# A scan followed by two gated layers: GpSimd adds the last three bits of all seventeen weight groups, and the order of work is drawn up anew

## The chip, the cores and the metric

The kernel runs on one core of one Trainium2 chip. The metric is the device time of one execution in microseconds (us): the median of three timed runs. One further execution was recorded by the hardware profiler, and all rows come from that one. In what follows PE is TensorE (PEld its weight loads), DVE is VectorE, ACT is ScalarE, POOL is GpSimd and SP is SyncE, which issues the transfers.

## The reference

A chunked linear recurrence over 768 steps for 4 batches of 8 heads makes `x`, 3072 tokens of 256 features. Two layers follow:

```python
h = x @ w_in                                   # 256 -> 2048
g = np.where(h > 0, h, np.exp(np.minimum(h, 0)) - 1)
x = g @ w_out                                  # 2048 -> 256
out = ((x @ w_a) * (x @ w_b)) @ w_out2         # 256 -> 1536 -> 256
```

[...]

## The kernel before

**The work.** Tokens are cut into 6 tiles of 512, and the recurrence into 24 units of 128 steps, 4 units to a tile. Stage A computes the first layer tile by tile: for each tile 8 pairs (`pair`), each with two blocks of 128 of the 2048 hidden features. A pair multiplies by `w_in` into PSUM (`up_a`, or `up_q` in the first two pairs, which take half a tile at a time), goes through ACT and DVE (`ex`, `em`, `gg`), and multiplies by `w_out` (`down`). Tile 0 multiplies by the whole 32-bit weights; from tile 1 on, weights and activations are split into a high and a low part of the faster type `fp32r` (`split`, `hi`, `lo`), and three products stand for one. Stage B computes the second layer for two tiles at a time in 18 groups (`group`).

**The units.** Each unit (`unit`) loads its data, scans on DVE (L678), multiplies on PE (`cbm2` L719, `ym` L766 to L774), masks on DVE (L735) and copies its result to `x0` on ACT (L806). For units 0 to 3 the scan reads a row that PE has spread over the partitions (`spread`, L654). GpSimd makes `xe` (L698), `sbd` (L750) and `cd` (L756) for them. Units 0 to 3 must be complete before tile 0 is.

**The weights.** There are 17 groups of 1024 columns: `w_in` and `w_out` have four each (numbers 0 to 7, in the order `w_in` 0, `w_out` 0, `w_in` 1, `w_out` 1, and so on), and `w_a`, `w_b` and `w_out2` three each (8 to 16). `weight` takes the two 32-bit words of each number through these steps: `load` (SP); `scale` (L523) on the upper word and `last3` (L536), which brings the top three bits of the lower word down to the end, both on ACT as the order stands; `shift` (L528) and `sign` (L531) on DVE; and `put` (L541), an integer addition that adds those last three bits. `PUT_DVE[n]` names the engine of the `put` of group n: 0 is GpSimd, 1 is VectorE, 2 either. VectorE has it for n = 2, 4 and 6, which are `w_in` 1, 2 and 3. Tile 0 multiplies by the result `m` directly: `w_in` 1 from pair 2 on (blocks 4 to 7), `w_in` 2 from pair 4, `w_in` 3 from pair 6.

**The order.** Each engine works through a queue in the order in which instructions were issued to it. `Plan` draws the order up when the kernel is built. Each step has its engines with an estimated cost, the steps it depends on, a due time, and for some a time before which it may not start. The planner repeatedly takes the step that could start first, in slots of 0.25 us, and among these the one with the lowest due time. It treats the port that DVE and POOL share as held by one of them at a time, for steps with `port=True`, of which `put` is one. `MOVE` adds an amount to due times, under "" for a whole part and by a step's name for one step. Where PE would wait early in the plan, `plan.fill` issues small multiplications of zeros (`warm`, L417) to fill the wait.

Of the kernel before, what the change touches and what calls it, by code (L numbers as in the profile page):

```python
# [35 lines left out]

LO_DVE = [[0, 1, 0, 1, 0, 1, 0, 1]] * NTILE

PUT_DVE = [0, 0, 1, 0, 1, 0, 1, 0, 0, 0, 0, 0, 0, 0, 0, 0, 0]
REST_DVE = [1, 1, 1, 1, 0, 1, 0, 1, 1, 0, 1, 0, 1, 0, 1, 0, 1]  # L40

T1, PAIR1, PAIR, GROUP = 25.0, 8.0, 6.2, 14.96
# [4 lines left out]


MOVE = {
    ("bc", (0, 1, 1)): {"": 7.7, "cast": 5.0},  # L50
    ("bc", (0, 2, 0)): {"": -5.4, "load": 2.3, "rest": -6.3},
# [4 lines left out]
    ("group", 1): {"dn_h": -2.5, "dn_l": -2.0, "lo": 6.2, "mm3": -0.9},  # L56
    ("group", 10): {"": 4.8, "hi": -4.1, "lo": -1.1},
    ("group", 11): {"ad": -4.1},
    ("group", 14): {"dn_l": -0.8, "lo": -5.3, "mm3": 1.4},
    ("group", 16): {"": 0.6},  # L60
    ("group", 17): {"dn_l": 1.7, "mm3": -2.1},
    ("group", 2): {"gg": -0.9, "mm3": 1.1},
    ("group", 3): {"dn_h": -1.4, "dn_l": 2.8, "lo": 2.7, "mm3": 1.7},
    ("group", 4): {"": 0.8, "hi": -2.2, "lo": 1.7, "mm3": 2.5},
    ("group", 5): {"": -8.2, "cp": 0.2, "dn_h": 0.5},
    ("late", 0): {"comb": 2.6},
    ("late", 1): {"": 0.1},
    ("late", 3): {"": -10.3},
    ("late", 4): {"high": 3.0},
    ("late", 5): {"": 3.5, "high": 9.5},  # L70
    ("late", 6): {"": 8.5, "high": -13.9},
    ("late", 7): {"": -14.4, "comb": 10.6},
    ("late", 8): {"": 0.3, "high": -6.8},
    ("pair", (0, 0)): {"": -7.7},
    ("pair", (0, 5)): {"": -2.6},
    ("pair", (0, 7)): {"": 2.8},
    ("pair", (1, 0)): {"": 4.8},
    ("pair", (1, 2)): {"up_a": 1.7},
    ("pair", (1, 7)): {"up_a": -1.9},
    ("pair", (2, 0)): {"": -10.6, "gg": 1.7},  # L80
    ("pair", (2, 1)): {"": 3.4, "up_a": -1.2},
    ("pair", (2, 2)): {"": 6.9},
    ("pair", (2, 3)): {"": -2.2, "dn_l": -1.2},
    ("pair", (2, 4)): {"": 1.7, "hi": -4.5, "lo": 3.7},
    ("pair", (2, 5)): {"": -3.8, "dn_l": -5.9, "lo": -0.2, "up_a": -2.2},
    ("pair", (2, 6)): {"": -4.1},
    ("pair", (2, 7)): {"up_a": -5.2},
    ("pair", (3, 2)): {"": 6.7, "dn_h": -3.4},
    ("pair", (3, 3)): {"": 4.4, "dn_h": -2.6},
    ("pair", (3, 4)): {"": 5.2, "up_a": -1.9},  # L90
    ("pair", (3, 5)): {"": -15.0, "dn_h": 2.3, "up_a": 1.0},
    ("pair", (3, 6)): {"": 6.9, "dn_h": -4.6, "up_a": -1.4},
    ("pair", (3, 7)): {"": 6.8, "dn_h": 13.1},
    ("pair", (4, 0)): {"": 9.0},
    ("pair", (4, 1)): {"": -11.8},
    ("pair", (4, 3)): {"": -11.1, "dn_h": -2.5, "dn_l": 3.6},
    ("pair", (4, 4)): {"": -0.6, "up_a": 5.5},
    ("pair", (4, 6)): {"dn_l": -5.5, "hi": 3.0},
    ("pair", (4, 7)): {"": -5.4, "em": 2.7, "up_a": -1.2},
    ("pair", (5, 0)): {"": 5.7},  # L100
    ("pair", (5, 1)): {"up_a": -3.1},
    ("pair", (5, 3)): {"up_a": -7.0},
    ("pair", (5, 4)): {"up_a": 0.1},
    ("pair", (5, 5)): {"": 5.8},
    ("pair", (5, 6)): {"": 4.7, "up_a": -6.5},
    ("pair", (5, 7)): {"": -0.7, "dn_h": 3.4},
    ("split", ("w_in", 0)): {"high": -20, "rest": -2.9},
    ("split", ("w_in", 1)): {"": -1.8, "high": -2.8},
    ("split", ("w_in", 3)): {"": 6.1, "high": 3.2},
    ("split", ("w_out", 0)): {"": 1.5},  # L110
    ("split", ("w_out", 1)): {"": -8.2},
    ("unit", 0): {"": 8.5, "ld0": -15.4, "ld_x": -9.9, "mask": -5.0},
    ("unit", 1): {"ld0": 7.0, "ld_x": 13.0},
    ("unit", 10): {"ld_a": -20, "st_bd": -5.0},
    ("unit", 11): {"scan": 6.0, "st_up": 8.5},
    ("unit", 12): {"": -12.6, "ld_a": 5.9},
    ("unit", 13): {"": -7.7, "<lambda>": 3.6, "scan": -4.3},
    ("unit", 14): {"": -0.6, "ld_sm": 4.0, "scan": -2.6, "st_bd": -4.2},
    ("unit", 15): {"": -3.8, "<lambda>": 11.8, "cbm": 6.9, "ld_a": 18.7, "scan": 5.9},
    ("unit", 16): {"": -8.1, "st_bd": -7.0},  # L120
    ("unit", 17): {"": -9.6, "last_col": 17.8},
    ("unit", 18): {"scan": 6.9, "st_bd": 10.0},
    ("unit", 19): {"": 6.4, "cbm": 8.3, "st_bd": -16.1},
    ("unit", 2): {"ld0": 12.2},
    ("unit", 20): {"": -4.8, "<lambda>": -18.3, "ld_db": -6.6, "ld_x": -2.5, "scan": 9.0},
    ("unit", 21): {"": 5.1, "ld_x": -4.6, "mask": 8.5, "scan": -4.0},
    ("unit", 22): {"<lambda>": 14.0, "cbm": -2.1, "ld_a": -9.9, "scan": 1.5, "x_lo": 15.3},
    ("unit", 23): {"mask": 7.9, "scan": 4.2, "st_bd": -12.9},
    ("unit", 3): {"ld_x": 12.1},
    ("unit", 5): {"last_col": 16.9, "x_hi": 20},  # L130
    ("unit", 6): {"": 2.8, "<lambda>": 6.4, "ld_a": -5.0, "ld_x": 2.7},
    ("unit", 7): {"": 3.0, "<lambda>": -1.2, "ld_a": -1.9, "ld_x": -3.6, "st_bd": -0.4},
    ("unit", 8): {"": 10.9, "ld_a": -7.3, "scan": -4.6, "st_up": 6.9, "x_lo": 3.9, "xend": -3.1},
    ("unit", 9): {"": 2.0, "ld_a": -3.0, "ld_sm": 2.5},
    ("w", ("w_in", 1)): {"shift": -19.7},
    ("w", ("w_in", 2)): {"put": 8.6},
    ("w", ("w_in", 3)): {"": 4.1, "scale": 7.8},
    ("w", ("w_out", 1)): {"put": -20, "sign": -11.6},
    ("w", ("w_out", 2)): {"sign": -6.5},
    ("w", ("w_out", 3)): {"load": -16.2, "sign": 4.2},  # L140
    ("wb", ("w_a", 0)): {"": -0.2, "last3": 7.5, "load": 0.2},
    ("wb", ("w_a", 1)): {"": -11.5},
    ("wb", ("w_a", 2)): {"": 12.0, "shift": -2.6, "sign": -2.6},
    ("wb", ("w_b", 0)): {"": -8.4, "scale": -20, "sign": -6.0},
    ("wb", ("w_b", 1)): {"": -8.8, "last3": 18.2, "shift": 18.2},
    ("wb", ("w_b", 2)): {"": 10.0, "last3": -3.0, "load": 7.0, "sign": 15.3},
    ("wb", ("w_out2", 0)): {"": 4.1, "sign": -9.5},
    ("wb", ("w_out2", 1)): {"sign": 6.5},
    ("wb", ("w_out2", 2)): {"last3": 13.0, "load": 16.4, "put": 10.3, "scale": 12.6, "shift": -0.1, "sign": -3.4},
    ("xset", 1): {"": -11.8, "x_h": -13.3, "x_l": 0.9},  # L150
}


# [13 lines left out]
class Plan:  # L167
# [12 lines left out]
    def add(self, engines, fn, *after, due, port=False, pad=0.0, weight=1.0, nb=0.7):  # L180
        flat = []
        name = fn.__name__
        move = MOVE.get(self.part, {})
        move = move.get("", 0.0) + move.get(name, 0.0)
        due, nb = due + move, nb + move if nb != 0.7 else nb
        self.parts.append((self.part, name))
        for a in after:
            flat += a if isinstance(a, list) else [a]
        self.steps.append((engines, fn, [a for a in flat if a is not None], due, port, pad, weight, nb))
        return len(self.steps) - 1  # L190
# [96 lines left out]
def kernel(  # L287
# [205 lines left out]
    def weight(name, g, due, now=True):  # L493
# [54 lines left out]
        wm[key] = m  # L548
        i_m[key] = add(({"POOL": 2.5}, {"DVE": 1.32}, {"DVE": 1.32, "POOL": 2.5})[PUT_DVE[n]], put, i4, i5, due=due, port=True)
        rb.users += [i1, i4, i_m[key]]  # L550
# [949 lines left out]
```

## Time and profile before

| quantity | value |
| --- | --- |
| timed runs, median (lowest to highest) | 619.58 us (619.28 to 619.68) |
| the profiled execution: its time, its span | 619.26 us, 617.2 us |
| busy: PE, DVE, ACT, POOL | 610.4, 393.8, 372.5, 332.4 us |
| mean granted clock of TensorE | 0.999 |

The span runs from the first instruction to the last, and 2.06 us of the execution's time lie outside it. PE's multiplications overlap and their ends are modelled, so that a busy PE may still be one that does less than it could. The chain of waits tells better when PE was held up by another engine.

### The profile page before, as it was taken

How to read it: one execution, taken by the hardware profiler on the slowest of the kernel's cores; microseconds unless marked ns; L12 is line 12 of the kernel's file. 1: busy time of each engine (PE TensorE's matmuls, PEld its weight loads, DVE VectorE, ACT ScalarE, POOL GpSimd, SP SyncE). 2: the span in 40 equal slices, each digit the busy share in tenths (PEclk: the TensorE clock that was granted, in tenths of full speed). 3: DMA queues.
4: the chain of work that ended last, by engine and by line, in shares of the span. 5: the costliest groups of instructions: out<-in, count | busy, mean ns of one | idle time of the engine just before them, and what ended most of it. 6: DMA issues, size and time to landing. Idle time of an engine off the chain costs nothing.

```text
span 617.2 us, 9444 instructions
## 1 busy us (share of the span) xinstructions
PE 610.4 (99%) x3627; PEld 482.3 (78%) x3627; DVE 393.8 (64%) x534; ACT 372.5 (60%) x529; POOL 332.4 (54%) x250
## 2 busy tenths in 40 slices
PE   9999999999999999999999999999999999999997
PEld 8875457778787877877888888888888888888885
DVE  7878768788778878878545647656533446433334
ACT  3555767766776766657777555556555556545453
POOL 2423367565555564356354576666655666555542
PEclk9999999999999999999999999999999999999999
DMA  7949633676677836410000000000100000100001
GB/s 230 308 171 306 204 95 125 229 251 234 206 256 249 293 107 214 135 52 0 2 1 1 1 0 1 0 1 1 69 0 2 0 1 0 70 0 1 1 0 68
DMA packets 33404, 59.94 MB, mean 97 GB/s; under 512 B 2736, under 2 KB 13904, under 8 KB 33360
## 3 DMA queue, kind: packets, MB, share of 16 engines
q1 hardware_dynamic: 33360, 59.35, 29.4%
q8 instruction: 28, 0.46, 0.3%
q14 instruction: 16, 0.13, 0.1%
HBM read 47.61 MB, written 11.73 MB: 96 GB/s over the span
## 4 chain that ended last, share of the span: by engine, by line
PE 98%; DVE 0%; ACT 0%; issue 0%; POOL 0%; POOLq 0%
PE acc L857 6%; PE acc L853 6%; PE up L841 6%; PE up L842 6%; PE acc L854 6%; PE up L844 6%; PE up L1183 5%; PE up L1182 5%; PE up L1186 5%; PE up L832 5%; PE acc L832 5%; PE acc L1243 4%; PE acc L1242 4%; PE acc L1244 4%; PE ybank L1243 3%; PE cbank L1243 3%
## 5 line engine op out<-in xcount | busy, mean ns | idle before, releaser
L1271 DVE TENSOR_TENSOR x<-x 128x512 f32<-128x512 f32 x36 | 30.3, 847 | 68.0 <-POOL x L1315 67.6
L940 ACT ACTIVATE e<-up 128x1024 f32<-128x1024 f32 x44 | 45.1, 1026 | 40.6 <-PE up L844 27.8
L1277 POOL TENSOR_TENSOR gl<-x,gh 128x512 fp32r<-128x512 f32 x35 | 48.4, 1385 | 37.7 <-ACT gh L1274 34.4
L961 POOL TENSOR_TENSOR gl<-e,gh 128x1024 fp32r<-128x1024 f32 x20 | 50.9, 2547 | 27.9 <-ACT gh L954 21.9
L1315 POOL TENSOR_TENSOR x<-e,x 128x512 f32<-128x512 f32 x36 | 46.8, 1316 | 34.1 <-ACT e L1254 33.3
L853 PE MATMUL acc<-gh,hi_w_out 128*128 128x512 f32 x160 | 63.5, 397 | 0.0
L854 PE MATMUL acc<-gh,lo_w_out 128*128 128x512 f32 x160 | 62.4, 390 | 0.0
L944 ACT ACTIVATE e<-e,bias 128x1024 f32<-128x1024 f32 x44 | 50.8, 1153 | 0.9
L857 PE MATMUL acc<-gl,hi_w_out 128*128 128x512 f32 x160 | 51.1, 396 | 0.0
L678 DVE TENSOR_TENSOR_SCAN ab<-ab,delta 128x512 f32<-128x512 f32 x36 | 50.1, 1410 | 1.2 <-DMA ab<-a_seg 1.2
L541 POOL TENSOR_TENSOR m<-m,raw 128x1024 int32<-128x1024 int32 x11 | 26.8, 2433 | 25.7 <-DVE m L531 11.4
L841 PE MATMUL up<-xh,hi_w_in 128*128 128x512 f32 x96 | 39.3, 409 | 0.0
L950 DVE SCALAR_TENSOR_TENSOR up<-e,up 128x512 f32<-128x512 f32 x40 | 27.7, 694 | 17.7 <-ACT e L944 17.0
L1262 DVE TENSOR_TENSOR p<-acc,p 128x512 f32<-128x512 f32 x36 | 24.3, 688 | 21.7 <-PE acc L1244 19.3
L1183 PE MATMUL up<-gh,lo_w_out 128*128 128x512 f32 x96 | 37.5, 391 | 0.0
L1182 PE MATMUL up<-gh,hi_w_out 128*128 128x512 f32 x96 | 37.5, 391 | 0.0
L950 DVE SCALAR_TENSOR_TENSOR e<-e,up 128x512 f32<-128x512 f32 x48 | 30.6, 678 | 10.8 <-ACT e L944 10.8
L1262 DVE TENSOR_TENSOR x<-acc,x 128x512 f32<-128x512 f32 x36 | 23.9, 685 | 21.3 <-PE acc L1244 21.2
L842 PE MATMUL up<-xh,lo_w_in 128*128 128x512 f32 x96 | 37.4, 390 | 0.0
L1274 ACT CAST gh<-x 128x512 fp32r<-128x512 f32 x36 | 22.4, 622 | 24.4 <-DVE x L1271 24.4
L1277 POOL TENSOR_TENSOR gl<-p,gh 128x512 fp32r<-128x512 f32 x18 | 23.9, 1331 | 21.8 <-issue 21.8
L853 PEld LDWEIGHTS acc<-gh,hi_w_out 128*128 128x128 f32 x160 | 30.1, 188 | 6.0
(306 smaller groups left out, 1733.7 us busy)
## 6 DMA issues: line engine op xcount, KB each, us to landing
ab<-a_seg SPq DMA_DIRECT2D x18, 512.0 KB
parts<-raw SPq DMA_DIRECT2D x64, 128.0 KB
sm<-parts SPq DMA_DIRECT2D x16, 512.0 KB
p<-in_xb SPq DMA_DIRECT2D x20, 256.0 KB
raw<-in_w_out SPq DMA_DIRECT2D x4, 1024.0 KB
fx<-in_w_out SPq DMA_DIRECT2D x3, 1024.0 KB
out_t<-m SPq DMA_DIRECT2D x12, 256.0 KB
raw<-in_w_in SPq DMA_DIRECT2D x2, 1024.0 KB
```

The lines of the kernel that those rows point to most:

```text
L832: nc.tensor.matmul(ps, w_mm(name, wm, f, c), src, start=start, stop=stop)
L841: nc.tensor.matmul(ps, w_mm(name, whi, f, c), xh[:, c, :], start=(c == 0), stop=False)
L842: nc.tensor.matmul(ps, w_mm(name, wlo, f, c), xh[:, c, :], start=False, stop=False)
L853: nc.tensor.matmul(accs[m], w_mm(name, whi, f, m), gh, start=(f == 0), stop=False)
L854: nc.tensor.matmul(accs[m], w_mm(name, wlo, f, m), gh, start=False, stop=False)
L857: nc.tensor.matmul(accs[m], w_mm(name, whi, f, m), gl, start=False, stop=(f == last))
L950: nc.vector.scalar_tensor_tensor(u[:, k, :] if on_dve else gf[:, k, :], gf[:, k, :], 0.0, u[:, k, :], op0=ALU.min, op1=ALU.max)
L961: nc.gpsimd.tensor_sub(gl.ap, gf, gh.ap.bitcast(F32))
L1182: nc.tensor.matmul(a4[m].ap, w_mm("w_out2", whi, f, m), gh, start=first, stop=False)
L1183: nc.tensor.matmul(a4[m].ap, w_mm("w_out2", wlo, f, m), gh, start=False, stop=False)
L1243: nc.tensor.matmul(bk.ap, lo_, x[:, 0], start=False, stop=False, **on)
L1277: eng[e].tensor_sub(tap("l" + w), tap(wa), tap("h" + w).bitcast(F32))
```

## The change

`PUT_DVE` is now zero for all groups: GpSimd does every `put`, among them the three that VectorE did. `MOVE` is replaced as a whole by another table, so that due times all over the kernel differ. No function, cost estimate or dependence changes. The core of the diff, with the lines that the prediction speaks of:

```diff
-PUT_DVE = [0, 0, 1, 0, 1, 0, 1, 0, 0, 0, 0, 0, 0, 0, 0, 0, 0]
+PUT_DVE = [0] * 17
...
-    ("pair", (0, 0)): {"": -7.7},
+    ("pair", (0, 0)): {"": -9.3},
...
-    ("unit", 0): {"": 8.5, "ld0": -15.4, "ld_x": -9.9, "mask": -5.0},
-    ("unit", 1): {"ld0": 7.0, "ld_x": 13.0},
-    ("unit", 2): {"ld0": 12.2},
-    ("unit", 3): {"ld_x": 12.1},
+    ("unit", 0): {"ld0": -8.0},
+    ("unit", 1): {"": 1.9, "scan": -1.2},
+    ("unit", 2): {"": 16.2},
+    ("unit", 3): {"": -5.0, "ld_x": 10.5},
...
-    ("w", ("w_in", 1)): {"shift": -19.7},
-    ("w", ("w_in", 2)): {"put": 8.6},
-    ("w", ("w_in", 3)): {"": 4.1, "scale": 7.8},
+    ("w", ("w_in", 0)): {"last3": -2.0},
+    ("w", ("w_in", 1)): {"": -14.5, "load": 3.3, "scale": 18.2, "sign": 7.3},
+    ("w", ("w_in", 2)): {"shift": 5.3, "sign": 5.5},
+    ("w", ("w_in", 3)): {"": 8.4, "load": -1.6, "shift": 1.6},
+    ("w", ("w_out", 0)): {"": -13.7, "shift": -7.1},
...
```

The rest of the table has some 120 lines before and after, for the units of later tiles, the pairs, the splits, the weights of the second layer and the groups of stage B, with amounts of up to 20 on either side.

## Rows read from the trace of the kernel before

**Rows 1.** The page: busy time by engine; the chain that ended last, by engine.

```profile
PE 610.4 (99%) x3627; PEld 482.3 (78%) x3627; DVE 393.8 (64%) x534; ACT 372.5 (60%) x529; POOL 332.4 (54%) x250
...
PE 98%; DVE 0%; ACT 0%; issue 0%; POOL 0%; POOLq 0%
```

**Rows 2.** The chain in order of time: start us, length us, what.

```profile
24.95 1.94 PE up L832 x8
...
27.97 0.86 ACT e L944
...
29.22 0.28 ACT x L806
...
29.54 1.50 PE ybank L417 x24
31.04 1.78 PE up L832 x8
...
612.83 0.59 ACT m L1211
```

**Rows 3.** Groups by line, PE: busy us, mean ns, idle before with its releasers.

```profile
L417 PE MATMUL ybank<-zt 128*128 128x128 bf16 x135 | 10.1, 241 | 1.9 <-POOL zt L413 1.1 <-ACT x L806 0.8
```

**Rows 4.** Line 541, the put: lowest, median and highest ns, first and last start.

```profile
L541 POOL TENSOR_TENSOR m<-m,fx x3: 2398/2398/2400, 26.2 to 83.4; 128x1024 int32<-128x1024 int32 x3
L541 DVE CUSTOM_DVE_ANT_0 m<-fx,m x2: 1216/1220/1225, 31.6 to 56.1; 128x2048 uint16<-128x2048 uint16 x2
L541 DVE CUSTOM_DVE_ANT_0 m<-raw,m x1: 1192/1192/1192, 73.2 to 73.2; 128x2048 uint16<-128x2048 uint16 x1
```

**Rows 5.** Timeline of POOL: start us, length us, what, idle before with its releaser.

```profile
26.18 2.40 POOL L541 TENSOR_TENSOR m<-m,fx 128x1024 int32<-128x1024 int32 x1 [1.21 <-issue]
...
37.88 0.62 POOL L698 TENSOR_TENSOR xe<-p,le 128x256 f32<-128x256 f32 x1 [8.43 <-ACT le L693]
...
53.19 0.62 POOL L750 TENSOR_TENSOR sbd<-state,hmask 128x256 f32<-128x256 f32 x1 [3.74 <-PE ybank L766]
...
58.80 0.74 POOL L698 TENSOR_TENSOR xe<-f_lo_w_out,le 128x256 f32<-128x256 f32 x1 [4.58 <-ACT le L693]
...
74.22 0.68 POOL L698 TENSOR_TENSOR xe<-f_lo_w_out,le 128x256 f32<-128x256 f32 x1 [5.44 <-ACT le L693]
```

**Rows 6.** Timeline of DVE.

```profile
24.53 1.52 DVE L531 SCALAR_TENSOR_TENSOR m<-fx,m 128x1024 int32<-128x1024 int32 x1
25.97 0.68 DVE L735 TENSOR_TENSOR f_lo_w_out<-cbank,f_lo_w_out 128x512 f32<-128x512 f32 x1
...
27.17 1.97 DVE L528 TENSOR_SCALAR m<-m 128x1024 int32<-128x1024 int32 x1
...
30.36 1.22 DVE L531 SCALAR_TENSOR_TENSOR m<-fx,m 128x1024 int32<-128x1024 int32 x1
...
51.59 1.20 DVE L531 SCALAR_TENSOR_TENSOR m<-fx,m 128x1024 int32<-128x1024 int32 x1
...
56.13 1.22 DVE L541 CUSTOM_DVE_ANT_0 m<-fx,m 128x2048 uint16<-128x2048 uint16 x1
...
58.40 0.67 DVE L528 TENSOR_SCALAR m<-m 128x1024 int32<-128x1024 int32 x1
...
70.96 1.21 DVE L531 SCALAR_TENSOR_TENSOR m<-raw,m 128x1024 int32<-128x1024 int32 x1
```

**Rows 7.** Timeline of PE: where tile 0 comes to its later blocks.

```profile
39.03 1.98 PE L832 MATMUL up<-x,m 128*128 128x512 f32 x4
...
58.96 5.31 PE L832 MATMUL up<-x,m 128*128 128x512 f32 x12
...
64.20 0.43 PE L766 MATMUL ybank<-f_lo_w_out,sbd 128*32 128x128 f32 x8
...
77.01 1.88 PE L832 MATMUL up<-x,m 128*128 128x512 f32 x4
```

**Rows 8.** Timeline of ACT: the first step of `w_out` 0.

```profile
17.44 1.14 ACT L523 ACTIVATE m<-fx 128x1024 f32<-128x1024 f32 x1 [2.09 <-DMA fx<-in_w_out]
```

More of the change, by code (lines that the diff above doesn't have):

```diff
@@ L49 @@
 MOVE = {
-    ("bc", (0, 1, 1)): {"": 7.7, "cast": 5.0},
-    ("bc", (0, 2, 0)): {"": -5.4, "load": 2.3, "rest": -6.3},
[4 rows of a table removed]
[L56 to L73, printed above, removed]
-    ("pair", (0, 0)): {"": -7.7},
-    ("pair", (0, 5)): {"": -2.6},
-    ("pair", (0, 7)): {"": 2.8},
@@ L77 @@
[L77 to L111, printed above, removed]
@@ L112 @@
-    ("unit", 0): {"": 8.5, "ld0": -15.4, "ld_x": -9.9, "mask": -5.0},
-    ("unit", 1): {"ld0": 7.0, "ld_x": 13.0},
[L114 to L120, printed above, removed]
@@ L121 @@
-    ("unit", 17): {"": -9.6, "last_col": 17.8},
-    ("unit", 18): {"scan": 6.9, "st_bd": 10.0},
-    ("unit", 19): {"": 6.4, "cbm": 8.3, "st_bd": -16.1},
-    ("unit", 2): {"ld0": 12.2},
[L125 to L128, printed above, removed]
@@ L129 @@
-    ("unit", 3): {"ld_x": 12.1},
[L130 to L134, printed above, removed]
-    ("w", ("w_in", 1)): {"shift": -19.7},
-    ("w", ("w_in", 2)): {"put": 8.6},
-    ("w", ("w_in", 3)): {"": 4.1, "scale": 7.8},
@@ L138 @@
[L138 to L150, printed above, removed]
+    ("bc", (0, 1, 0)): {"": -5.4},
+    ("bc", (0, 2, 0)): {"": -9.9, "rest": -7.9},
+    ("bc", (0, 2, 1)): {"rest": -9.9},
+    ("bc", (1, 2, 0)): {"": -6.8, "cast": 16.2},
+    ("bc", (1, 2, 1)): {"": 3.0, "cast": 3.2, "rest": 5.8},
@@ new lines @@
+    ("group", 0): {"": -2.1, "cp": 1.5, "dn_1": 0.9, "dn_h": 2.3, "dn_l": 2.2, "mm3": -2.4},
+    ("group", 1): {"": -9.0, "gg": 3.0, "lo": 11.1, "mm3": -1.0},
+    ("group", 10): {"mm3": -0.8},
+    ("group", 11): {"lo": 1.9},
+    ("group", 17): {"dn_h": 4.2},
+    ("group", 2): {"dn_h": -2.3, "dn_l": -4.2},
+    ("group", 4): {"": 2.7, "gg": 1.4},
+    ("group", 5): {"dn_l": -1.5},
+    ("group", 6): {"": -6.8},
+    ("late", 0): {"": -6.2, "high": 3.2},
+    ("late", 1): {"": 16.7, "comb": -5.2, "high": 3.2},
@@ new lines @@
+    ("late", 3): {"": 2.7, "comb": -6.0, "high": 3.2, "high_s": 7.0, "rest_s": 5.0},
+    ("late", 5): {"": -3.1, "high": -7.9},
+    ("late", 6): {"": 6.0, "rest": 0.6},
+    ("late", 7): {"": -17.6, "high": 8.0},
+    ("late", 8): {"": 0.4, "high": -2.9},
+    ("pair", (0, 0)): {"": -9.3},
+    ("pair", (0, 3)): {"": 6.9},
+    ("pair", (0, 4)): {"": -3.9, "dn_w": 5.2},
+    ("pair", (1, 2)): {"up_a": 2.8},
+    ("pair", (1, 4)): {"": -2.8},
+    ("pair", (1, 5)): {"": -6.3, "dn_h": 1.7},
+    ("pair", (1, 6)): {"": -6.0},
@@ new lines @@
+    ("pair", (2, 0)): {"": -11.5},
+    ("pair", (2, 1)): {"dn_h": -0.2, "dn_l": -1.6},
+    ("pair", (2, 2)): {"lo": 4.1},
+    ("pair", (2, 3)): {"": 2.5, "dn_l": -0.9},
+    ("pair", (2, 4)): {"": 6.5, "dn_l": -3.2, "lo": 3.7},
+    ("pair", (2, 5)): {"": -10.0, "em": 4.9},
+    ("pair", (2, 6)): {"": -4.3},
+    ("pair", (3, 1)): {"": 2.1},
+    ("pair", (3, 3)): {"dn_h": -1.1},
+    ("pair", (3, 4)): {"": 5.2},
+    ("pair", (3, 5)): {"": -18.0},
+    ("pair", (3, 6)): {"dn_h": -3.1, "up_a": -1.1},
@@ new lines @@
+    ("pair", (3, 7)): {"dn_h": 14.4},
+    ("pair", (4, 0)): {"": 3.6},
+    ("pair", (4, 1)): {"": -18.1},
+    ("pair", (4, 3)): {"": -3.8},
+    ("pair", (4, 4)): {"": -5.2, "dn_h": -1.2},
+    ("pair", (4, 5)): {"": 4.8, "dn_h": 1.7},
+    ("pair", (4, 6)): {"": 2.8, "up_a": -2.4},
+    ("pair", (4, 7)): {"up_a": -1.8},
+    ("pair", (5, 1)): {"": -3.7},
+    ("pair", (5, 2)): {"": 13.2},
+    ("pair", (5, 6)): {"": 5.0},
+    ("split", ("w_in", 0)): {"": -4.8, "high": -15.7, "rest": 3.1},
@@ new lines @@
+    ("split", ("w_in", 3)): {"": 5.8, "high": 5.5},
+    ("split", ("w_out", 0)): {"": 9.6, "high": -11.1},
+    ("split", ("w_out", 2)): {"": -5.5},
+    ("unit", 0): {"ld0": -8.0},
+    ("unit", 1): {"": 1.9, "scan": -1.2},
+    ("unit", 11): {"": 1.9, "scan": 5.5, "ym": -7.9},
+    ("unit", 12): {"": -19.8, "ld_a": 20},
+    ("unit", 13): {"": -12.1, "mask": -5.6},
+    ("unit", 14): {"st_bd": -4.0},
+    ("unit", 15): {"cbm": -3.7, "ld_x": -1.8, "mask": -10.3},
+    ("unit", 16): {"": -2.5, "last_col": 16.5, "mask": 4.1, "st_bd": -18.9},
@@ new lines @@
+    ("unit", 17): {"": -6.5, "ym": 3.2},
+    ("unit", 18): {"": -16.0, "st_bd": 18.9},
+    ("unit", 19): {"": 3.3, "ld_a": -7.5, "x_lo": -10.5},
+    ("unit", 2): {"": 16.2},
+    ("unit", 20): {"": -4.9, "mask": 10.7},
+    ("unit", 21): {"cbm": -4.8, "st_bd": -3.0, "x_lo": 6.2, "ym": -10.4},
+    ("unit", 22): {"": -17.0, "mask": -11.1, "scan": -4.5},
+    ("unit", 23): {"cbm": -5.8, "ld_a": 4.2, "mask": 16.6, "scan": 2.1},
+    ("unit", 3): {"": -5.0, "ld_x": 10.5},
+    ("unit", 4): {"": -6.5},
@@ new lines @@
+    ("unit", 5): {"": -1.0, "ld_db": 6.8, "ld_x": 13.1, "scan": 2.8},
+    ("unit", 6): {"": 5.2, "<lambda>": 10.3, "ld_a": -7.9, "scan": 5.0},
+    ("unit", 7): {"": 3.8, "ld0": -3.1, "ld_a": -3.5, "ld_db": -7.0, "ld_x": -2.6, "scan": 1.1},
+    ("unit", 8): {"": 11.2, "ld_a": -9.6, "ld_db": 1.8, "st_bd": 4.2},
+    ("unit", 9): {"": 2.0, "ld_a": -8.3, "ld_x": -0.6, "mask": -11.4},
+    ("w", ("w_in", 0)): {"last3": -2.0},
+    ("w", ("w_in", 1)): {"": -14.5, "load": 3.3, "scale": 18.2, "sign": 7.3},
@@ new lines @@
+    ("w", ("w_in", 2)): {"shift": 5.3, "sign": 5.5},
+    ("w", ("w_in", 3)): {"": 8.4, "load": -1.6, "shift": 1.6},
+    ("w", ("w_out", 0)): {"": -13.7, "shift": -7.1},
+    ("w", ("w_out", 1)): {"": -16.7, "put": -1.0, "sign": -20},
+    ("wb", ("w_a", 0)): {"": -0.2, "load": 0.2},
+    ("wb", ("w_a", 1)): {"load": -3.0},
+    ("wb", ("w_a", 2)): {"": 20, "load": 2.2, "put": 0.3},
+    ("wb", ("w_b", 0)): {"": -9.4, "load": 15.2},
+    ("wb", ("w_b", 1)): {"": -8.0, "last3": 14.5},
+    ("wb", ("w_b", 2)): {"": 5.7, "sign": 13.5},
@@ L151 @@
+    ("wb", ("w_out2", 0)): {"": 7.4, "scale": -5.5, "shift": -5.4},
+    ("wb", ("w_out2", 1)): {"scale": 3.0, "sign": 5.0},
+    ("wb", ("w_out2", 2)): {"": 9.5},
+    ("xset", 1): {"": 5.7, "f_t2": 9.0, "f_t3": 6.5},
+    ("xset", 2): {"": 10.5, "f_t3": -2.8},
 }
```

4 rows, old and new, of the table MOVE are left out of this document.

## Prediction

> **What bounds the kernel now.** I read the page first, then the chain of waits in order of time, then the timelines of the engines around each of the three additions that move. The page says that PE is busy for 99% of the span and that 98% of the chain that ended last is PE [rows 1]. By itself a busy PE proves little, since its ends are modelled. The chain proves more: its last piece on another engine before the end is ACT's copy of unit 3's result, 29.22 to 29.50 us. After it come 24 multiplications of zeros and then, at 31.04, the first pair-1 product; from there to ACT's last copy at 612.83 I found no piece of any other engine [rows 2]. So the kernel has two parts. Until 31.04 us PE waits for the recurrence of units 0 to 3. From 31.04 to 612.83, 581.8 us, it works through its products with nothing in between, and the rest is a tail that this change doesn't touch.
>
> It follows where time can be won and where lost. The 581.8 us shrink only if PE gets fewer products, and it gets the same ones. What a new order can shorten is the start. PE's fills of zeros and its idle time before them are 10.1 and 1.9 us [rows 3], nearly all before 31.04. That is 12 us of waiting, most of it for data that must first land, be scanned and masked. Lost time can come anywhere: any step that becomes late for PE adds its lateness.
>
> **The change part by part.** *VectorE loses three additions*: 2 x 1.22 + 1.19 = 3.63 us [rows 4]. DVE is no releaser in the chain after 31.04, so that time by itself is worth nothing at the end.
>
> *GpSimd gains three*, at 2.40 us each, 7.2 us together [rows 4]; the form and shape are those of the additions it already does, so there is no unknown here. What they cost is a matter of when `m` is complete. I keep the old order, put each addition on POOL directly behind its `sign`, and compare with the product that needs it.
>
> For `w_in` 1, `sign` ends at 30.36 + 1.22 = 31.58 [rows 6]. POOL has been idle for 8.43 us until 37.88 [rows 5], so the addition ends at 33.98. Block 4 starts at 39.03 [rows 7]: 5.0 us to spare.
>
> For `w_in` 2, `sign` ends at 52.79 [rows 6], and POOL, idle for 3.74 us, takes up `sbd` at 53.19 [rows 5]. Ahead of that, the addition ends at 55.19, earlier than VectorE's does (56.13 + 1.22 = 57.35 [rows 6]). Block 8 starts at 58.96 [rows 7]: 3.8 us to spare where VectorE had 1.6. `sbd` comes 2.0 us later, at 55.19; the product that reads it starts at 64.20 [rows 7], so this too is hidden. Behind `sbd` the addition would end at 53.81 + 2.40 = 56.21, with 2.7 us to spare.
>
> For `w_in` 3, `sign` ends at 72.17 [rows 6]; POOL has been idle for 5.44 us until 74.22 [rows 5]. The addition ends at 74.57, block 12 starts at 77.01 [rows 7]: 2.4 us to spare, and `xe` moves by 0.35 us. So the three together cost PE nothing; the cover is 5.0, 3.8 and 2.4 us, and the bound above is what is left when it is used up (a rival, below).
>
> *The shared port.* While POOL adds, DVE may be held. A row shows it: the `shift` that starts at 27.17 under POOL's addition of 26.18 to 28.58 takes 1.97 us, where the same form takes 0.67 at 58.40 [rows 5, 6]. That is 1.3 us for one addition. Three make 3.9 us, against the 3.63 that DVE is relieved of; the lower bound is nothing, where only masks or `gg`, which read PSUM, stand beside the addition. I take 1.3 each: DVE is left as loaded as it was, and nothing is won there.
>
> The Trainium skill (SBUF — State Buffer, Who interferes with whom) has a rule that speaks against the change: DVE and GpSimd share one pair of ports as an exclusive lock, and a DVE instruction with two inputs in SBUF is fully held for the whole length of a GpSimd instruction that reads SBUF. By that rule each addition could hold a scan or a `sign` for all of its length, 7.2 us for three, twice what DVE is relieved of; the `shift` above agrees, since it ended 0.56 us after the addition did.
>
> *The due times.* Here the trace of before has no price, only bounds. The three additions' predecessors move: `w_in` 1 has its load due at 9.8 instead of 21 and free to start from -0.2 instead of 11, its `scale` at 32.7 instead of 29, `shift` at 14.5 instead of 9.3, `sign` at 21.8 instead of 29 and `put` at 14.5. `w_out` 0 has its load due at 7.3 instead of 21 and no longer held until 11, and its `shift` at 8.2 instead of 29. On SP both pass only loads of units from 4 on; those of units 0 to 3 still stand ahead of them, and those of unit 3 now ahead of unit 2's. Unit 2 as a whole goes from -16 to 0.2 and unit 3 from -9 to -14, but unit 3's `spread` still takes over the PSUM of unit 2's, so the serial run of spread, scan, spread, scan stays.
>
> The gain is bounded by what was lost just before 31.04. Unit 3's first mask began at 25.97, right behind a `sign` of `w_out` 0 that DVE had taken up at 24.53; PE had gone from `cbm2` to the next product at 24.95 [rows 2, 6], so the mask could have begun about then: 1.0 us. ACT's `em`, on the chain at 27.97, held unit 3's copy back until after it, and then the 24 fills stood ahead of pair 1 although the copy had ended at 29.50: 1.5 us [rows 2]. That makes at most 2.5 us to win. An earlier `w_out` 0 could remove the first loss, because ACT waited 2.09 us for that load, until 17.44 [rows 8]; but the rows ahead of it on SP are as many as before. The loss is bounded by the same steps standing the other way round: two more steps of DVE ahead of the masks, 1.2 + 0.7, some 1.9 us [rows 6]. The planner's rule and its costs are unchanged in the start, and the predecessors of each step too, so I take the value nearest to the rows of before: 0, give or take 0.6.
>
> **The sum.** 619.26 us of the profiled execution + 0 (additions) + 0 (port) + 0 (due times) = 619.26. The median of the timed runs, 619.58, lies 0.32 higher; the forecast for a median is 619.5. A change below 0.2%, 1.24 us, is about what measuring this kernel can't tell from none.
>
> **The rivals.** *Absorbed, my forecast (0.50).* PE's run from about 31 us to the end stays closed: 618.4 to 620.7, its own range.
>
> *The start shortens (0.24).* The fills ahead of pair 1 go, and the masks of unit 3 no longer stand behind a weight step: 1.5 to 2.5 us less, about 617.5. For it: all this time is waiting, and the new dues reach into these steps. Against it: the fills come from the planner's own estimate of the wait, which has not changed, and half of the gain depends on a queue that is as long as before.
>
> *A GpSimd queue makes PE wait (0.20), on the slower side.* The place is `w_in` 2. POOL works in order; if the new order puts the addition behind unit 7's `xe`, which waits for ACT until 58.80 [rows 5], it starts at 58.80 + 0.74 = 59.54 and ends at 61.94. Block 8, due at 58.96, would start 3.0 us late, and PE has no other product ahead of it: 619.58 + 3.0 = 622.6, or less if PE can be given the scan's products first, about 621.5. The mechanism decides from the point where the addition ends after 58.96, that is starts after 56.56. For it: the new `put` of `w_in` 2 has no early due time of its own, its `shift` and `sign` are due over 5 us later, and 2.4 us is a long step in a queue with waits. Against it: the planner sees these waits, and POOL has room there.
>
> *The port holds the recurrence (0.06).* An addition of POOL stands beside a unit's two scans and holds each to its end, up to 2.4 us, of which the units' own slack covers most; 1.3 us reaches PE, 620.9. The exclusive lock that the Trainium skill (SBUF — State Buffer, Who interferes with whom) describes would work this way. Against it: the planner keeps additions and scans apart.
>
> **How the numbers follow.** The likeliest case gives 619.5. Two in ten may be left out: the range goes down to 617.4, which takes in the shorter start but for its best tenths, and up to 621.8, which takes in the port and the milder half of the queue case. Faster by over 0.2%: the start case less a little, 0.23. Slower: the queue case, half of the port case and a little of my own, 0.25. Within: 0.52.
>
> **What would show it.** Line 541 should show 17 additions on POOL at 2.4 us and none on DVE; POOL's busy time up by 7.2 us to about 339.6, DVE's by between -3.6 and +0.3. The chain of waits should leave the other engines for good at 30.4 to 31.6 us. If block 8 starts directly behind an addition on POOL, the queue case is right; if pair 1 starts before 30 us, the start case is. A chain with pieces of DVE, ACT or POOL after 100 us would make the prediction wrong in a way that I did not price: a due time in stage A or B that comes too late for PE.

## The result and the profile after

The changed kernel takes 623.06 us (median of 5 runs, 622.13 to 624.52), the kernel before 619.51 us: a ratio of 1.0061 with a 95% interval from 1.0043 to 1.0079. It is slower by 0.6%, where no change that can be told was forecast, and it lies above the range of 617.4 to 621.8. The profiled execution is one of the longer ones, 624.20 us with a span of 622.5 us. Lines of the changed kernel are six lower than before: the addition is L535, `up_mm` L826 and L835 to L838.

The page, busy time and chain by engine, beside [rows 1]:

```profile
PE 612.8 (98%) x3627; PEld 483.1 (78%) x3627; DVE 393.1 (63%) x519; ACT 374.6 (60%) x533; POOL 349.5 (56%) x261
...
PE 93%; DMA 2%; POOL 1%; ACT 1%; DVE 1%; issue 1%; SPq 0%; POOLq 0%; ACTq 0%
```

PE has the same 3627 products. The chain is no longer PE's alone: 93% where it was 98%, and transfers, GpSimd, ScalarE and VectorE have entered. The additions by line, beside [rows 4], and where the three that moved stand on POOL:

```profile
L535 POOL TENSOR_TENSOR m<-m,raw x12: 2400/2440/3236, 16.1 to 274.5; 128x1024 int32<-128x1024 int32 x12
L535 POOL TENSOR_TENSOR m<-m,fx x5: 2400/2788/3197, 27.0 to 82.0; 128x1024 int32<-128x1024 int32 x5
```

```profile
32.57 3.19 POOL L535 TENSOR_TENSOR m<-m,fx 128x1024 int32<-128x1024 int32 x1 [2.25 <-ACT raw L530]
...
52.27 2.79 POOL L535 TENSOR_TENSOR m<-m,fx 128x1024 int32<-128x1024 int32 x1 [1.93 <-DVE m L525]
...
71.27 2.41 POOL L535 TENSOR_TENSOR m<-m,raw 128x1024 int32<-128x1024 int32 x1 [1.24 <-DVE m L525]
```

They end at 35.76, 55.06 and 73.68 us. PE comes to the blocks that need them at 39.93, 57.62 and 75.24 us, so none is late. The chain in order of time, beside [rows 2]:

```profile
4.55 2.90 PE acc L648 x16
...
30.40 1.50 PE ybank L411 x24
...
32.99 1.92 PE up L826 x8
...
128.09 4.05 DMA sm<-parts
132.15 1.26 DVE gl L953 x2
...
138.41 2.35 POOL gl L955
...
156.24 2.37 POOL gl L955
...
172.40 4.50 DMA raw<-in_ct
...
180.62 0.70 DVE ab L729
...
430.92 0.69 DVE c L1265
```

The start is what it was: the same fills, the same steps, 0.86 us later because the first products of `spread` took longer in this execution, and unit 4's `cbm2` now ahead of pair 1 for 1.09 us, which PE has to do anyway. So pair 1 starts at 32.99 us where it started at 31.04. What is new begins at 128 us. The timelines of PE, POOL, DVE and ACT at two of these places:

```profile
131.66 0.71 PE L851 MATMUL acc<-gl,hi_w_out 128*128 128x512 f32 x2
133.56 0.47 PE L835 MATMUL up<-xh,hi_w_in 128*128 128x512 f32 x1 [1.19 <-DVE gl L953]
...
179.80 0.61 PE L851 MATMUL acc<-gl,hi_w_out 128*128 128x512 f32 x2
181.36 0.38 PE L726 MATMUL cbank<-sm 128*128 128x128 bf16 x4 [0.94 <-DVE ab L729]
```

```profile
128.72 2.43 POOL L535 TENSOR_TENSOR m<-m,raw 128x1024 int32<-128x1024 int32 x1
```

```profile
129.91 2.32 DVE L672 TENSOR_TENSOR_SCAN ab<-ab,delta 128x512 f32<-128x512 f32 x1 [0.59 <-DMA ab<-a_seg]
132.15 1.26 DVE L953 TENSOR_TENSOR gl<-up,gh 128x512 fp32r<-128x512 f32 x2
```

```profile
176.92 0.62 ACT L573 CAST raw<-raw 128x512 bf16<-128x512 f32 x1 [4.18 <-DMA raw<-in_ct]
```

At 132 us PE wants the PSUM bank that DVE's low part `gl` still reads. DVE has put a scan of unit 11 ahead of it. That scan waited 0.59 us for its data and then took 2.32 us, where others take 1.2, beside an addition of `w_a` 0 on POOL, which is on POOL in both kernels. At 181 us PE waits for a mask; ahead of it ACT stood for 4.18 us before a `cast` whose load had not landed, with the steps that PE needed behind it.

I count a wait as the time from one product's start to the next, less what the same pair of products takes elsewhere: 133.56 - 131.66 - 0.55 = 1.35 us at 132 us, and in the same way 0.57 near 141, 0.47 near 158, 1.10 at 181 and 0.28 near 431. Together 3.8 us, about the 3.55 between the medians; with the start 0.86 us later in this execution it is 4.6 of the 5.3 us between the spans.

### The profile page after: what moved, and what is told of

It is laid out like the page before. It is cut to its first block, busy times and chain, and to the rows that moved or that the text cites. A ratio compares the mean times of both kernels' runs of the same rounds, so it can differ in the third digit from the quotient of the medians.

```text
span 622.5 us, 9445 instructions
## 1 busy us (share of the span) xinstructions
PE 612.8 (98%) x3627; PEld 483.1 (78%) x3627; DVE 393.1 (63%) x519; ACT 374.6 (60%) x533; POOL 349.5 (56%) x261
## 4 chain that ended last, share of the span: by engine, by line
PE 93%; DMA 2%; POOL 1%; ACT 1%; DVE 1%; issue 1%; SPq 0%; POOLq 0%; ACTq 0%
PE up L835 6%; PE acc L851 5%; PE up L836 5%; PE up L838 5%; PE up L1180 5%; PE acc L847 5%; PE up L1177 5%; PE up L1176 5%; PE acc L848 5%; PE up L826 5%; PE acc L826 5%; PE acc L1237 4%; PE acc L1236 4%; PE acc L1238 4%; PE cbank L1236 3%; PE ybank L1237 3%
## 5 line engine op out<-in xcount | busy, mean ns | idle before, releaser
L672 DVE TENSOR_TENSOR_SCAN ab<-ab,delta 128x512 f32<-128x512 f32 x36 | 54.8, 1542 | 2.2 <-DMA ab<-a_seg 2.0
L835 PE MATMUL up<-xh,hi_w_in 128*128 128x512 f32 x96 | 39.4, 410 | 1.2 <-DVE gl L953 1.2
L535 POOL TENSOR_TENSOR m<-m,raw 128x1024 int32<-128x1024 int32 x12 | 30.0, 2499 | 18.6 <-DVE m L525 14.6
L851 PEld LDWEIGHTS acc<-gl,hi_w_out 128*128 128x128 f32 x160 | 29.2, 188 | 7.1 <-POOL gl L955 1.3
L848 PEld LDWEIGHTS acc<-gh,lo_w_out 128*128 128x128 f32 x160 | 30.1, 188 | 5.8
```

What stands on the lines that cost most here:

```text
L672: nc.vector.tensor_tensor_scan(lt[:, h4].rearrange(flat), lt[:, h4].rearrange(flat) if n else flat4(sp[g]), delta.rearrange(flat), 0.0, op ...
L835: nc.tensor.matmul(ps, w_mm(name, whi, f, c), xh[:, c, :], start=(c == 0), stop=False)
L848: nc.tensor.matmul(accs[m], w_mm(name, wlo, f, m), gh, start=False, stop=False)
L851: nc.tensor.matmul(accs[m], w_mm(name, whi, f, m), gl, start=False, stop=(f == last))
```

## The experiments

Theory A: the time is lost to the order, which the planner drew up anew from new due times and from GpSimd's estimate for three additions; the additions on GpSimd themselves cost nothing. Theory B, the rival: the additions cost it, by the shared port or by being late. Line numbers shift in each kernel by the lines that its edit adds. In some experiments the order is kept and only a step is taken elsewhere. For these `HOLD` names steps by their number in the plan; such a step is issued after the one it is mapped to:

```diff
+        self.kept = []
...
                 if go:
-                self.steps[i][1](e)
...
+                if i in HOLD:
+                    self.kept.append((i, e))
+                else:
+                    self.steps[i][1](e)
+                    for h in [h for h in self.kept if HOLD[h[0]] == i]:
+                        self.kept.remove(h)
+                        self.steps[h[0]][1](h[1])
```

**The additions alone, in the old order.** On the kernel before:

```diff
         def put(e):
-            eng[e].tensor_tensor(out=mi, in0=mi, in1=low, op=ALU.add)
+            on = nc.gpsimd if n in (2, 4, 6) else eng[e]
+            on.tensor_tensor(out=mi, in0=mi, in1=low, op=ALU.add)
```

> The kernel before with its order of all steps as it was; only the three additions of w_in 1, 2 and 3 are issued on GpSimd, each at the place in the order where VectorE's stood. Theory A (the new order costs the time, the additions nothing): 619.5 us, within 0.6 us of before, and no piece of another engine in the chain between 35 and 600 us. Theory B (the additions on GpSimd cost the time, by the shared port or by lateness): most of the 3.5 us, so 622 to 623.5 us, with PE waiting before 100 us.

Measured: 619.14 us beside 619.44, a ratio of 0.9994 (0.9985 to 1.0002). The chain in order of time and two of the moved additions on POOL:

```profile
29.97 0.28 ACT x L807
...
31.79 1.78 PE up L833 x8
...
613.54 0.59 ACT m L1212
```

```profile
54.92 2.41 POOL L542 TENSOR_TENSOR m<-m,fx 128x1024 int32<-128x1024 int32 x1
...
73.00 3.25 POOL L542 TENSOR_TENSOR m<-m,raw 128x1024 int32<-128x1024 int32 x1 [3.47 <-DVE m L531]
```

Between 31.79 and 613.54 us the chain has no piece of another engine, as in [rows 2]. In the old order the three additions cost nothing that can be told from noise: by the interval at most 0.1 us. Theory B, which needed most of 3.5 us there, has fallen.

**The additions put back, in the new order.** The same edit on the changed kernel with `nc.vector`.

> The changed kernel with its order of all steps as it is; only the three additions of w_in 1, 2 and 3 are issued on VectorE, each at the same place in the order. Theory A: as the changed kernel, 622 to 624.5 us, with PE's waits near 132, 141, 158 and 181 us still there (1.35 + 0.57 + 0.47 + 1.10 = 3.5 us). Theory B: 619.5 to 620.5 us.

Measured: 625.21 us, 1.0084 (1.0071 to 1.0097), more than expected. With VectorE adding, the new order is no faster, and 2 us slower at that. The waits near 132 and 181 us are there, and one of 1.9 us at 154. POOL and DVE ahead of that one:

```profile
150.97 2.42 POOL L536 TENSOR_TENSOR m<-m,raw 128x1024 int32<-128x1024 int32 x1
```

```profile
151.07 3.40 DVE L673 TENSOR_TENSOR_SCAN ab<-ab,delta 128x512 f32<-128x512 f32 x1
```

An addition of `w_b` 0, on GpSimd in every kernel here, began 0.10 us ahead of a scan of unit 13, and the scan took 3.40 us instead of 1.2. The profile of the changed kernel has no such meeting; the wait behind it is about the 2 us between the two medians, though that rests on one profile of each.

**Only an estimate changed.** On the kernel before, engines and due times as they are:

```diff
-i_m[key] = add(({"POOL": 2.5}, {"DVE": 1.32}, {"DVE": 1.32, "POOL": 2.5})[PUT_DVE[n]], put, i4, i5, due=due, port=True)
+i_m[key] = add(({"POOL": 2.5}, {"DVE": 1.62}, {"DVE": 1.32, "POOL": 2.5})[PUT_DVE[n]], put, i4, i5, due=due, port=True)
```

> The kernel before with its due times and its engines, all three additions on VectorE; only the planner's estimate of VectorE's addition is 1.62 instead of 1.32 us, so that the order is drawn up anew from the first of them on. Theory A (due times fit one order, and any order drawn up anew from them is worse, whatever engine adds): slower than before by 1 to 8 us, 621 to 628 us, with waits of PE spread over stage A. Theory B (it takes GpSimd's additions to lose the time): 619.5 us.

Measured: 627.78 us, 1.0137 (1.0123 to 1.0151). No addition has changed its engine, and the kernel loses 8 us. Who waited for whom, PE's waits:

```profile
PE up L841 <- DVE gl L959: 2.7, 3, 1.4
...
PE cbank L732 <- DVE ab L735: 0.9, 1, 0.9
PE acc L854 <- DVE lo_w_out L485: 0.8, 1, 0.8
```

The first number is the total, then how often, then the longest. The chain leaves PE near 82 to 103, 153 to 170, 220 to 228 and 303 to 314 us. This speaks for theory A: with the due times of the kernel before, the one order has no waits after the start, and an order that differs by one estimate has six. It is one such redrawing; the next run is a second.

**The old due times with all additions on GpSimd.** On the kernel before, `PUT_DVE = [0] * 17`, the order drawn up anew.

> The kernel before with its own table of due times, and all additions given to GpSimd, so that the planner draws up the order anew from there. Theory A: the order differs from the first moved addition on, and due times fitted to the one order no longer fit the other: anything from 619.5 to 624 us, most likely some 621, with waits of PE after 35 us at places that have nothing to do with the additions. Theory B: 622 to 623.5 us, with waits at the additions.

Measured: 627.63 us, 1.0132 (1.0117 to 1.0147), beyond the 624 expected at most. This is the change without its new table. The longest of PE's waits on another engine:

```profile
PE ybank L719 <- DVE xl L812: 2.5, 1, 2.5
```

None of PE's waits in this profile is on an addition. The new table has won back 4.6 of these 8.2 us, and 3.5 are left.

**Four places of the new order turned.** On the changed kernel:

```diff
+HOLD = {397: 436, 452: 467, 400: 467, 492: 513, 497: 513, 590: 567, 591: 567}
```

> The changed kernel with the order kept but for four places, where a step that waits is put behind the step that PE needs: VectorE's scan of unit 11 behind the low part of pair 5 of tile 1; GpSimd's cd of unit 12 and xe of unit 11 behind the low part of pair 6; GpSimd's xe and sbd of unit 13 behind the low part of pair 0 of tile 2; ScalarE's cast of the last piece of C behind the high part of pair 4 and unit 14's copy. Theory A: the waits near 132, 141, 158 and 181 us go, 3.5 us in all: 619.3 to 620.3 us. Theory B: none of these steps is one of the three additions, so 622 to 624 us.

Measured: 620.68 us, 1.0026 (1.0015 to 1.0037), 12 runs from 620.10 to 623.88. Some 2.4 of 3.5 us are back, so most of the loss lay in these places. None of the steps is one of the three additions. The profiled execution was a long one, 622.58 us, and shows a wait that the changed kernel's profile does not have. POOL, DVE and PE:

```profile
149.18 2.43 POOL L547 TENSOR_TENSOR m<-m,raw 128x1024 int32<-128x1024 int32 x1
```

```profile
149.28 3.41 DVE L684 TENSOR_TENSOR_SCAN ab<-ab,delta 128x512 f32<-128x512 f32 x1
152.61 1.25 DVE L956 SCALAR_TENSOR_TENSOR e<-e,up 128x512 f32<-128x512 f32 x2
```

```profile
154.01 0.47 PE L847 MATMUL up<-xh,hi_w_in 128*128 128x512 f32 x1 [1.97 <-DVE e L956]
```

The addition of `w_b` 0 began 0.10 us ahead of unit 13's second scan; the scan took 3.41 us instead of 1.2 and ended 1.08 us after the addition did, so it was held for nearly all of it. The gate behind it came late for PE, by 1.97 us. In the changed kernel's own profile the addition came after the scan, and there was no wait:

```profile
152.64 2.44 POOL L535 TENSOR_TENSOR m<-m,raw 128x1024 int32<-128x1024 int32 x1
```

The plan sets the two one after the other, but no wait between the engines enforces it. GpSimd's step just ahead of the addition waited for a transfer in both profiles, until 151.56 and until 148.75 us, and the scans waited for another: which comes first is decided by when data land.

**One addition later.** On the changed kernel `HOLD = {473: 406}`.

> The changed kernel with one step moved: GpSimd's addition for w_a 0 (which is on GpSimd before and after) goes behind the sbd and cd of unit 11. If the shared port is what makes the wait at 132 us, the scan of unit 11 takes 1.2 us again where it took 2.32, and PE's wait there falls from 1.35 to about 0.25 us: some 622.0 us. If the late transfer of the scan's data makes it, nothing changes at 132 us: 623 us.

Measured: 622.16 us, 1.0042 (1.0029 to 1.0056). DVE and PE:

```profile
128.51 1.23 DVE L684 TENSOR_TENSOR_SCAN ab<-ab,delta 128x512 f32<-128x512 f32 x1 [0.18 <-DMA ab<-a_seg]
129.65 1.26 DVE L965 TENSOR_TENSOR gl<-up,gh 128x512 fp32r<-128x512 f32 x2
```

```profile
131.21 0.40 PE L847 MATMUL up<-xh,hi_w_in 128*128 128x512 f32 x1
```

The scan takes 1.23 us again, and PE's wait is gone. Of the 1.35 us, 1.1 are what the scan took longer beside the addition, so most of the wait at 132 us was the port; the scan's data were also less late, by 0.4 us. The median falls by 0.9 us beside the changed kernel's of another run; the intervals overlap, so the place is shown by the rows rather than by the median.

**One cast later.** On the changed kernel `HOLD = {590: 567, 591: 567}`.

> The changed kernel with one place turned: ScalarE's cast of the last piece of C, which waits for its load, goes with its store behind the high part of pair 4 and unit 14's copy. Theory A: the wait of 1.10 us near 181 us goes and nothing else: 621.5 to 622.4 us. Theory B: 623 us.

Measured: 622.97 us, 1.0052 (1.0038 to 1.0066). The wait at 181 us is gone from the profile, and the median has not moved: this profile has the meeting of scan and addition near 150 us instead, with a wait of 1.2 us behind it. A single place can't be read from the total here.

**More places turned.** The four places, with `489: 511, 490: 511, 1467: 1473` added.

> The changed kernel with the four places of the run before turned, and two more: VectorE's two scans of unit 13 behind the gate of pair 0 of tile 2, and in stage B the gate of product 22 of group 5 behind that of product 21. Theory A, with the shared port as part of it (a scan that meets a GpSimd addition is held for all of it, which cost 1.97 us at 153 us in the profile of the run before, and does so in some executions only): the rest goes too, 619.4 to 620.0 us, and the runs lie closer together. Theory B': what is left above the kernel before is something else than these waits, so again 620.5 us or more.

Measured: 622.71 us, 1.0039 (1.0026 to 1.0052), where at most 620.0 was expected, and no better than with four places; the two intervals overlap. The two scans, now behind the gate, met the addition there all the same and made masks late, and the chain names the low part on POOL next. Stretches of this kernel (the stretch, its length, the busy time of PE, PEld, DVE, ACT and POOL with their instructions, then the granted clock, the share of the transfers and GB/s):

```profile
154.00:157.00 3.00, 1.38 (x8) 0.84 (x7) 1.76 (x4) 3.00 (x5) 2.42 (x2) 1.00 0.79 238
157.00:161.00 4.00, 3.78 (x47) 2.80 (x48) 2.66 (x5) 2.75 (x5) 3.80 (x6) 0.57 0.42 144
```

After a stretch in which PE was busy for 1.38 of 3 us, the granted clock was 0.57 for 4 us, so most of them were at the lower of the two levels, 1.2 GHz. In this profile the waits cost more than their own length.

**The gate without the scans.** The four places, with `1467: 1473` added.

> The changed kernel with the four places turned, and in stage B the gate of product 22 of group 5 behind that of product 21; the scans of unit 13 stay where they are. Theory A: as with the four places, less 0.3 us for the wait near 429 us: 620.0 to 620.6 us, and single executions 2 us longer when GpSimd's addition for w_b 0 comes before the second scan of unit 13. If the scans of unit 13 were not what spoiled the run with six places: 622 us or more.

Measured: 621.82 us, 1.0035 (1.0022 to 1.0047), runs from 620.70 to 622.59. The wait that stood near 431 us in the changed kernel's profile is gone. The one wait of PE on another engine after the start is 1.1 us near 151 us, behind the same scan, which took 3.41 us again. The median is above the 620.0 to 620.6 us expected; the profiled execution, 620.71 us, is one of the two shortest, and has the meeting all the same.

**Only the second scan later.** With `490: 511` added to that.

> The changed kernel with the four places and the gate in stage B turned as in the run before the last, and one scan more: only the second scan of unit 13, which met GpSimd's addition for w_b 0 in that run's profile (3.41 us instead of 1.2), goes behind the gate of pair 0 of tile 2. If that meeting at the shared port is what is left, PE waits for no engine between 35 us and the end, the executions lie within 1 us of each other, and the kernel takes 619.4 to 620.2 us. If turning scans only moves the wait, as with the two scans before, 621 us or more.

Measured: 620.74 us, 1.0022 (1.0013 to 1.0032). PE's waits on other engines after the start:

```profile
PE acc L863 <- POOL gl L967: 0.7, 1, 0.7
...
PE ybank L772 <- POOL sbd L756: 0.4, 1, 0.4
```

The wait at 151 us is gone, and two stand near 157 us in its place, together 1.1 us as well. The median lies between the two expectations, and its interval overlaps those of the runs with four places and with the gate. So the order can be brought to within 0.3% of the kernel before by hand; the last of it is not found.

**The start, which I had priced as the gain.** On the kernel before, the fill ahead of step 90, pair 1's first product, is left out:

```diff
-                    self.fill(m)
+                    if i not in (90,):
+                        self.fill(m)
```

> The kernel before with its order and engines; only the 24 multiplications of zeros ahead of the first product of pair 1 are left out, which no result uses. If the start is worth its time at the end: pair 1 starts at 29.6 instead of 31.04 us and the kernel takes 618.0 us. If the time is given back, because weights and scans of tile 0 are then late for PE: pair 1 starts early all the same, PE waits before 100 us, and the kernel takes 619 us or more.

Measured: 618.20 us, 0.9976 (0.9968 to 0.9985). The second kernel leaves out the fill ahead of step 70 too and has `HOLD = {81: 69, 83: 69, 76: 72}`.

> The kernel before with all that I had priced at 2.5 us in the start: the fills ahead of unit 3's products and of pair 1 left out, unit 3's masks ahead of the sign and the addition of w_out 0, and unit 3's copies ahead of pair 0's em on ScalarE. If the start is worth its time: pair 1 starts at 28.6 us and the kernel takes 617.0 us. If it is given back: 618.5 us or more, with PE's waits before 100 us.

Measured: 616.60 us, 0.9953 (0.9941 to 0.9965). The chain of the one and of the other:

```profile
28.74 0.28 ACT x L807
29.07 1.99 PE up L833 x8
...
611.07 0.59 ACT m L1212
```

```profile
28.44 0.29 ACT x L819
28.77 1.99 PE up L845 x8
...
611.00 0.59 ACT m L1224
```

Pair 1 follows unit 3's copy directly, and nothing stands in the chain behind it until the end. From pair 1 to ACT's last copy it is 582.0 and 582.2 us, beside the 581.8 of before, so the time won in the start is kept nearly whole. The medians fall by 1.6 and 3.2 us, for the 1.5 and 2.5 that the rows of before gave; by the interval of the second, 2.2 to 3.7, the 2.5 may well be right. The second is faster than both kernels.

## Why the prediction was wrong

The step that failed is the term for the due times, 0 give or take 0.6. I bounded it by what the start could win or lose and took the rest of the order for as closed as [rows 2] show it. It measured 3.5 us, at five places from 128 us on and none in the start, where nothing was won or lost but by the execution. The text names this case at its end, a due time in stage A or B that comes too late for PE, and gives it no price and no chance. The 581.8 us without a wait in [rows 2] I read as room, and they were the state of one order. An order redrawn from the same due times lost 8 us through an estimate changed by 0.3 us. One sign was also read off wrongly: the chain of before leaves the other engines at 29.50 us, and the 30.4 to 31.6 us that I gave for it are about the start of pair 1, at 31.04.

The terms for the engines were right. VectorE's 3.63 us were worth nothing, and the three additions cost nothing: together they changed the time by 0.3 us to the good, which the interval doesn't tell from none. The spare times forecast as 5.0, 3.8 and 2.4 us came out as 39.93 - 35.76 = 4.2, 57.62 - 55.06 = 2.6 and 75.24 - 73.68 = 1.6 us in the new order. POOL's busy time rose by 17.1 us, not by 7.2: POOL has 11 instructions more, and only three of them are the additions; the others are steps that may run on either engine. And two of the three took longer than 2.40 us, 3.19 and 2.79.

The port's term was too small for one meeting and looked for at the wrong additions. I priced 1.3 us; a scan was held for 2.2 us of an addition of 2.43. The Trainium skill (SBUF — State Buffer, Who interferes with whom) says that the one that comes second is held for the other's whole length, and the rows at 149 us agree. The `shift` that I named beside this rule reads a single tensor, so that it is not the rule's case of two inputs; the scan is. The moved additions held scans too, as these two scans of DVE show, before and after:

```profile
32.75 2.33 DVE L678 TENSOR_TENSOR_SCAN f_hi_w_out<-f_hi_w_out,delta 128x512 f32<-128x512 f32 x2
```

```profile
32.35 4.49 DVE L672 TENSOR_TENSOR_SCAN f_hi_w_out<-f_hi_w_out,delta 128x512 f32<-128x512 f32 x2
```

PE did not wait for these. The additions that made PE wait are those of `w_a` 0 and `w_b` 0, which GpSimd does in both kernels.

Of the rivals, the one of a GpSimd queue named the sign for the wrong place: `w_in` 2 was never late, so its 622.6 us came near by luck. Its mechanism, a step that PE needs behind a waiting one, is what happened, but on VectorE, GpSimd and ScalarE alike and 70 us later. The rival of the port, at 0.06, has the mechanism of the wait at 132 us, and about its 1.3 us, by another addition; what spoke against it, that the planner keeps additions and scans apart, did not hold when data landed otherwise than planned. The start did not shorten, though the two experiments show that it can, by about as much as I gave it.

Open are the last 1 us or so above the kernel before, and which step near unit 13's late loads would have to go where. The loads themselves were not moved. Both redrawings come from one table of due times, so what an order drawn from another would lose is not shown.

## What to carry to other kernels

Where due times go with one order, price a change of any planner input as a new order: here it had 3.5 to 8 us to lose that the old trace couldn't show. Try the edit first with the old order held. Where one engine's work is closed from some point to the end, as PE's was here, time won ahead of that point is kept: both experiments on the start kept it nearly whole. Where two engines share a port, don't count on an order that only the plan knows: here it was kept in some executions and not in others.

## What the runs showed of the hardware

The first 16 products of `spread` took 2.90 us in the chain of the changed kernel and 2.03 in that of the kernel before, with the same instructions ahead of them and a granted clock of 1.00 shown for both stretches. It is not the order: the profile with the additions moved in the old order has 2.78 us, and the one with one addition later in the new order 1.84. This alone moved all that follows in the start by 0.9 us; the runs of the kernel before lie between 618.85 and 620.82 us. What makes it long or short is not shown.

A scan of 1.2 us that began 0.10 us behind an addition of GpSimd took 3.41 us and ended 1.08 us after it, so the two went one after the other. And the granted clock fell to 0.57 for the 4 us shown above, after a stretch in which PE had been busy for 1.38 of 3 us.
